# Chunks four to seven solved as two pairs on POOL, and their preparation and solving put above the weight conversions

## The chip, the cores and the metric

The kernel runs on one core of a Trainium2 chip. The core has five engines with a queue of their own each, and each takes its instructions strictly in the order in which they stand in that queue: TensorE (PE in the profile; its weight loads are PEld), VectorE (DVE), ScalarE (ACT), GpSimd (POOL) and SyncE (SP, which here only starts transfers). The metric is the device time of one execution in microseconds (us).

## The reference

Three layers follow each other. The first is a linear recurrence over 768 steps, for 4 x 8 = 32 heads with a 40 x 40 state each; the other two are feed-forward layers over the 3072 tokens that come out of it.

```python
for t in range(S):                                   # S = 768
    y[:, :, t] = einsum('bhd,bhde->bhe', r_t, state)
    Sa = einsum('bhde,bhe->bhd', state, a_t)
    state = state * w_t[:, :, None, :] - einsum('bhd,bhe->bhde', Sa, b_t) + einsum('bhd,bhe->bhde', v_t, k_t)
x = y as 3072 tokens x 320
h = x @ w_in                                         # 320 -> 2048
g = where(h >= 1, h, where(h <= -1, 0, (h + 1)**2 / 4))
x = g @ w_out                                        # 2048 -> 320
out = ((x @ w_a) * (x @ w_b)) @ w_out2               # 320 -> 1536 -> 320
```

Weights arrive as 64-bit floats and are taken apart on the chip into two 32-bit parts each, since a product is made of a high and a low part.

## The kernel before

**The recurrence** is cut into 24 chunks of 32 steps (C = 32). A chunk g passes through three routines:

- `prepare(g)` (line 113) needs no state, so it may run ahead. It loads `ein` (`load_e`), scans the decays on DVE (L127, L130), multiplies on POOL (L136, out `ein`), and multiplies on PE (L146, out `pab`) what DVE then masks into `lab` (L154); one part of it goes to DRAM as `amd` (L156). From chunk 4 on there is one buffer for `ein`, and the load of chunk g+1 is issued after the products of chunk g.
- A **solve** turns the 32 x 32 triangular matrix of each head of a chunk (`amd`) into its inverse (`xtd`). `solve(sb)` (line 203) does it for the four chunks of a block sb at once: 128 partitions are 4 chunks x 32 heads, and 30 rounds of two operations (L212 and L214, tiles `tm` and `apm`) run over all rows of the matrix. `solve_pair(i, eng)` (line 221) does it for two chunks, with the upper and the lower partitions each taking every second row: 31 rounds (L239, L241) over half as many rows. Before, chunks 0 and 1 are solved as a pair on DVE, chunks 2 and 3 as a pair on POOL, and all later ones in fours by `solve` on POOL.
- `core(g)` (line 285) carries the state on: products `pw` (L295), an ACT copy (`ws`, L298), products `pu` (L303) with the inverse `xtl` read back from `xtd` (`load_xt`), products `pss` (L314), whose result DVE scales into the next state (L317), and transposes `put` and `pst`. `outp(g)` and `x_out(g)` make the chunk's output and lay it into `xa`, the input of the first feed-forward layer, for two chunks at a time.

**The first feed-forward layer** (`ffn_block`, 12 blocks of two chunks) takes 16 pieces f a block: products `pha` (L588, L596), four operations on DVE, ACT and POOL, and products `ya`. It needs the converted weights. A **conversion** (`from_f64`, line 500) loads `raw`, and passes through DVE (L506, L507, L510, L511), ACT (L508, L509) and POOL (L512), then an ACT cast and a subtraction on POOL or DVE (L536, L546, L561). There are 36 of them for this layer. `p1_stage` (line 160) makes further tables for the chunks of a block, with two long scans on DVE (L178, L183) and two multiplications on POOL (L188, out `pkb`).

**The second feed-forward layer** (`pa`, `pb`, `po`) follows when the first is done.

**What sets the order:** the program is written as generators that a loop over chunks advances; a scheduler then puts every engine's instructions in order by a model of their times and by a priority, which is the place in the program moved by `tc.high_priority(offset=...)`. The conversions have an offset of -900 (line 447), the pieces of the first feed-forward layer -8000 (line 486); prepare, solve and core have none. The table `side` says beside which chunk a generator is advanced. The order is fixed when the program is built: on the chip an engine that waits for its next instruction does nothing else.

Of the kernel before, what the change touches and what calls it, by code (L numbers as in the profile page):

```python
# [16 lines left out]
C = 32  # L17
# [7 lines left out]
def rwkv_moe_kernel(ctx: ExitStack, tc: tile.TileContext, r, k, v, w, a, b, w_in, w_out, w2a, w2b, w2o, ein, pin, vin, rin, vtin, out):  # L25
# [44 lines left out]
    def recurrence(ffn_block, xap, spare, conv, more_units, early):  # L70
# [7 lines left out]
        with ExitStack() as es:  # L78
# [142 lines left out]
            def solve_pair(i, eng):  # L221
# [3 lines left out]
                t = pre.tile([128, CW], F32, name="apm") if i == 0 else spare("wi1", F32)[:, 0:CW]  # L225
                N = t[:, 0:C * C].rearrange("p (j i) -> p j i", i=C)
                X = t[:, 2:CW].rearrange("p (q i) -> p q i", i=2 * C + 2)[:, :, 0:C]
                nc.sync.dma_start(out=t[:, 0:C * C], in_=amd[0][2 * i:2 * i + 2].rearrange("c k q s t -> (c k q) (s t)").unsqueeze(0)
# [5 lines left out]
                tm = None if i == 0 else spare("wo1", F32)  # L234
                for m in range(C - 1):
                    n, k = C - 1 - m, m // 2 + 1
                    tv = (pre.tile([128, 240], F32, name="tm") if i == 0 else tm)[:, 0:k * n].rearrange("p (j i) -> p j i", i=n)
                    rows = X[:, n2 - k:n2]
                    eng.tensor_tensor(out=tv, in0=rows[:, :, m:m + 1].to_broadcast([128, k, n]),  # L239
                                            in1=N[:, m, m + 1:].unsqueeze(1).to_broadcast([128, k, n]), op=ALU.mult)  # L240
                    eng.tensor_tensor(out=rows[:, :, m + 1:], in0=rows[:, :, m + 1:], in1=tv, op=ALU.add)  # L241
                    if m % 2:
                        yield
                nc.gpsimd.affine_select(out=X, in_=X, pattern=[[2, n2], [1, C]], base=2 - C, channel_multiplier=0,
                                        compare_op=ALU.is_ge, fill=0.0)
                for h in range(2):
                    nc.sync.dma_start(out=xtd[0][2 * i:2 * i + 2].rearrange("c k q (j h) t -> h (c k q) j t", h=2)[h, :, ::-1],
                                      in_=X[64 * h:64 * h + 64])
# [36 lines left out]
            def core(g):  # L285

                ru, nxt, lab, wc = RU[g % 2], RU[(g + 1) % 2], LAB[g % PL], WC[g % (PL + 1)]
                if g % 4 == 0 or g == 2:
                    load_xt(g)
# [18 lines left out]
                if (g + 1) % 4 and g + 1 != 2:  # L308
                    load_xt(g + 1)
# [71 lines left out]


# [5 lines left out]
            for sb in range(1, NSB):  # L388
                gen = p1_stage(sb)
                slots = [4 * sb - 4 + j for j in range(4)]  # L390
                for j in slots:
                    put(j, 1, (gen, 3 if j < slots[-1] else 99))
                gen = solve(sb)
                for j in range(2):
                    put(4 * sb - 2 + j, 1, (gen, 9 if j < 1 else 99))
            for g in range(NCH):
                put(g + 2, 0, (x_out(g), 99))
                if g >= 4:
                    put(max(g - PL, (g - 4) // 2), 0, (prepare(g), 99))
# [631 lines left out]
```

## Time and profile before

| | us |
|---|---|
| median of 3 runs | 1519.99 (1517.62 to 1527.1) |
| profiled execution | 1516.01 |
| its span, from the first to the last instruction | 1514.0 |
| PE, DVE, ACT, POOL busy | 1124.2, 712.3, 522.0, 667.4 |
| granted clock of TensorE, mean over the span | 0.926 |

The span is the stretch that the trace covers; the profiled execution's own time is 2.0 us longer. A share of busy time is an average over stages that have different limits, so the stages have to be looked at one by one.

### The profile page before, as it was taken

What the parts mean: (1) busy time and instruction counts of PE and PEld (TensorE: products, weight loads), DVE (VectorE), ACT (ScalarE), POOL (GpSimd) and SP (SyncE); (2) the same over time, 40 slices, a digit from 0 to 9 for tenths busy, and PEclk for the clock granted to TensorE, in tenths of its full rate; (3) what the DMA queues carried; (4) which work ended last, traced back from release to release, by engine and by line L of the source; (5) the groups of instructions that cost most, each with busy time, mean ns of one, the idle gap of its engine ahead of it and who ended that gap; (6) DMA issues with size and microseconds to landing.
All of it is one profiled execution on the core that took longest, in us unless ns stands there. A gap on an engine that the chain in (4) does not pass through costs nothing.

```text
span 1514.0 us, 42965 instructions
## 1 busy us (share of the span) xinstructions
PE 1124.2 (74%) x18674; PEld 1005.5 (66%) x18674; DVE 712.3 (47%) x1345; ACT 522.0 (34%) x1171; POOL 667.4 (44%) x866
## 2 busy tenths in 40 slices
PE   0102234457676888887889978879999999999996
PEld 0102123356565778776778867779988888888885
DVE  5975677873444555546554366784411111111110
ACT  1212424244222333333444456565422222222221
POOL 4647455785082583285248235465422222222221
PEclk9999999988657998898889988989999999999998
DMA  8746778665645334534443243441110010000000
GB/s 232 136 129 124 156 155 188 157 141 107 152 123 139 91 106 114 138 97 102 106 130 107 80 137 113 133 129 44 52 30 21 19 37 23 18 1 18 1 18 20
DMA packets 193626, 144.72 MB, mean 96 GB/s; under 512 B 138644, under 2 KB 168340, under 8 KB 190932
## 3 DMA queue, kind: packets, MB, share of 16 engines
q1 hardware_dynamic: 160276, 128.25, 33.6%
q10 hardware_dynamic: 33152, 13.64, 4.0%
q8 instruction: 148, 2.42, 0.7%
q14 instruction: 50, 0.41, 0.1%
HBM read 111.97 MB, written 29.88 MB: 94 GB/s over the span
## 4 chain that ended last, share of the span: by engine, by line
PE 49%; DMA 16%; DVE 16%; POOL 8%; issue 6%; ACT 3%; SPq 1%; ACTq 0%; POOLq 0%; DVEq 0%
PE pb L596 9%; PE pa L596 8%; PE po L596 8%; DMA ein<-in_ein_dram 6%; PE pha L596 6%; PE ya L596 6%; POOL apm L214 2%; POOL tm L212 2%; DMA raw<-in_moe_w_in_dram 2%; DVE cve L506 1%; PE ya L588 1%; DVE cvf L511 1%; PE pss L314 1%; DVE ewx L127 1%; PE pha L588 1%
## 5 line engine op out<-in xcount | busy, mean ns | idle before, releaser
L650 POOL TENSOR_TENSOR gl<-cl,gh 128x256 fp32r<-128x256 f32 x192 | 144.5, 764 | 194.7 <-ACT gh L648 162.3
L701 POOL TENSOR_TENSOR gl<-gf,gh 128x512 fp32r<-128x512 f32 x72 | 92.8, 1289 | 308.4 <-ACT gh L699 308.4
L596 PE MATMUL pha<-xa,wi 128*128 128x256 f32 x1239 | 194.8, 302 | 0.8 <-issue 0.8
L697 DVE TENSOR_TENSOR gf<-pb,asb 128x512 f32<-128x512 f32 x72 | 49.7, 691 | 305.6 <-PE pb L596 297.2
L596 PEld LDWEIGHTS pha<-xa,wi 128*128 128x128 f32 x1239 | 179.8, 211 | 1.0 <-issue 1.0
L596 PE MATMUL ya<-wo,gh 128*128 128x320 f32 x576 | 138.2, 325 | 2.2 <-ACT yo L913 2.2
L644 ACT ACTIVATE cl<-cl 128x256 f32<-128x256 f32 x192 | 75.5, 416 | 168.7 <-DVE cl L643 166.6
L303 PE MATMUL pu<-ws,xtl 32*32 32x40 f32 x1536 | 28.1, 239 | 132.3 <-DMA xtl<-xtd 88.5
L512 POOL TENSOR_TENSOR cvf<-cvf,cve 128x256 f32<-128x256 f32 (+2 forms) x84 | 75.8, 902 | 114.6 <-DVE cve L510 66.9
L643 DVE TENSOR_SCALAR cl<-pha 128x256 f32<-128x256 f32 x177 | 69.2, 417 | 115.8 <-PE pha L596 106.6
L596 PE MATMUL ya<-wo,gl 128*128 128x320 f32 x384 | 111.3, 331 | 6.4 <-POOL gl L650 5.7
L303 PEld LDWEIGHTS pu<-ws,xtl 32*32 32x32 f32 x1536 | 23.8, 141 | 135.5 <-issue 97.0
L596 PE MATMUL po<-wo,gh 128*128 128x320 f32 x504 | 108.9, 308 | 0.0
L596 PEld LDWEIGHTS ya<-wo,gh 128*128 128x128 f32 x576 | 104.5, 204 | 3.8 <-ACT yo L913 2.5
L648 ACT CAST gh<-cl 128x256 fp32r<-128x256 f32 x192 | 74.5, 404 | 51.6 <-DVE cl L646 36.5
L699 ACT CAST gh<-gf 128x512 fp32r<-128x512 f32 x72 | 44.7, 621 | 133.9 <-DVE gf L697 131.8
L214 POOL TENSOR_TENSOR apm<-apm,tm 128x30 f32<-128x30 f32 (+9 forms) x150 | 86.9, 579 | 8.9
L596 PE MATMUL pb<-wi,w 128*128 128x512 f32 x288 | 90.8, 396 | 0.0
L596 PE MATMUL pb<-wo,w 128*128 128x512 f32 x288 | 90.7, 396 | 0.0
L695 ACT COPY asb<-pa 128x512 f32<-128x512 f32 x72 | 42.2, 587 | 133.7 <-PE pa L596 133.7
L212 POOL TENSOR_TENSOR tm<-apm 128x30 f32<-128x30 f32 (+9 forms) x150 | 82.0, 547 | 8.9
L646 DVE TENSOR_TENSOR cl<-pha,cl 128x256 f32<-128x256 f32 x177 | 70.1, 418 | 31.3 <-ACT cl L644 30.8
(167 smaller groups left out, 2598.8 us busy)
## 6 DMA issues: line engine op xcount, KB each, us to landing
ein<-in_ein_dram SPq DMA_DIRECT2D x21, 838.9 KB
vut<-in_vtin_dram SPq DMA_DIRECT2D x24, 416.0 KB
ru<-in_vin_dram SPq DMA_DIRECT2D x48, 160.0 KB
kbi<-pwd SPq DMA_DIRECT2D x48, 160.0 KB
lg<-pwd SPq DMA_DIRECT2D x48, 160.0 KB
pkb<-in_pin_dram SPq DMA_DIRECT2D x11, 640.0 KB
pwd<-pkb SPq DMA_DIRECT2D x11, 640.0 KB
ptw<-in_pin_dram SPq DMA_DIRECT2D x6, 660.5 KB
```

The source lines that it names most:

```text
L212: nc.gpsimd.tensor_tensor(out=tv, in0=X[:, 0:m, m:m + 1].to_broadcast([128, m, n]), in1=X[:, m, m + 1:].unsqueeze(1).to_broadcast([128, m, ...
L214: nc.gpsimd.tensor_tensor(out=X[:, 0:m, m + 1:], in0=X[:, 0:m, m + 1:], in1=tv, op=ALU.add)
L303: nc.tensor.matmul(pu[q:q + C, j, :], lhsT=xt[q:q + C, j, :], rhs=ws[q:q + C, j, :], start=True, stop=True)
L512: nc.gpsimd.tensor_tensor(out=f, in0=f, in1=e.bitcast(F32), op=ALU.mult)
L596: nc.tensor.matmul(**p)
L643: nc.vector.tensor_scalar(out=cl, in0=ph, scalar1=-1.0, scalar2=1.0, op0=ALU.max, op1=ALU.min)
L644: nc.scalar.activation(out=cl, in_=cl, func=AF.Square, scale=0.5, bias=0.5)
L646: nc.vector.tensor_tensor(out=gf, in0=ph, in1=cl, op=ALU.max)
L648: nc.scalar.copy(out=gh, in_=gf)
L650: nc.gpsimd.tensor_tensor(out=gl, in0=gf, in1=gh.bitcast(F32), op=ALU.subtract)
L697: nc.vector.tensor_tensor(out=gf, in0=pb, in1=asb, op=ALU.mult)
L701: nc.gpsimd.tensor_tensor(out=gl, in0=gf, in1=gh.bitcast(F32), op=ALU.subtract)
```

## The change

Chunks 4 to 7 are no longer solved by one `solve(1)`, but by two calls of `solve_pair` on POOL, the first for chunks 4 and 5, the second for 6 and 7; they use the tiles `apm` and `tm` of `solve`. The pair reads `amd` and writes `xtd` of its own block, so the first can start when two chunks are prepared, not four. `load_xt(6)` moves to the start of core(6). A new wrapper `ahead(gen, n)` advances a generator with a raised priority: 3000 for the two pairs, 1500 for the preparation of chunks 4 to 7.

```diff
--- before.py
+++ after.py
@@ -222,19 +222,20 @@
 
 
                 n2 = C // 2
-                t = pre.tile([128, CW], F32, name="apm") if i == 0 else spare("wi1", F32)[:, 0:CW]
+                sb, c = divmod(2 * i, 4)
+                t = pre.tile([128, CW], F32, name="apm") if i != 1 else spare("wi1", F32)[:, 0:CW]
                 N = t[:, 0:C * C].rearrange("p (j i) -> p j i", i=C)
                 X = t[:, 2:CW].rearrange("p (q i) -> p q i", i=2 * C + 2)[:, :, 0:C]
-                nc.sync.dma_start(out=t[:, 0:C * C], in_=amd[0][2 * i:2 * i + 2].rearrange("c k q s t -> (c k q) (s t)").unsqueeze(0)
+                nc.sync.dma_start(out=t[:, 0:C * C], in_=amd[sb][c:c + 2].rearrange("c k q s t -> (c k q) (s t)").unsqueeze(0)
                                   .to_broadcast([2, 64, C * C]))
                 yield
                 for h in range(2):
                     nc.gpsimd.memset(t[64 * h:64 * h + 64, C + h:C * (C - 1) + h + 1:2 * C], 1.0)
                 yield
-                tm = None if i == 0 else spare("wo1", F32)
+                tm = None if i != 1 else spare("wo1", F32)
                 for m in range(C - 1):
                     n, k = C - 1 - m, m // 2 + 1
-                    tv = (pre.tile([128, 240], F32, name="tm") if i == 0 else tm)[:, 0:k * n].rearrange("p (j i) -> p j i", i=n)
+                    tv = (pre.tile([128, 240], F32, name="tm") if i != 1 else tm)[:, 0:k * n].rearrange("p (j i) -> p j i", i=n)
                     rows = X[:, n2 - k:n2]
                     eng.tensor_tensor(out=tv, in0=rows[:, :, m:m + 1].to_broadcast([128, k, n]),
                                             in1=N[:, m, m + 1:].unsqueeze(1).to_broadcast([128, k, n]), op=ALU.mult)
@@ -244,7 +245,7 @@
                 nc.gpsimd.affine_select(out=X, in_=X, pattern=[[2, n2], [1, C]], base=2 - C, channel_multiplier=0,
                                         compare_op=ALU.is_ge, fill=0.0)
                 for h in range(2):
-                    nc.sync.dma_start(out=xtd[0][2 * i:2 * i + 2].rearrange("c k q (j h) t -> h (c k q) j t", h=2)[h, :, ::-1],
+                    nc.sync.dma_start(out=xtd[sb][c:c + 2].rearrange("c k q (j h) t -> h (c k q) j t", h=2)[h, :, ::-1],
                                       in_=X[64 * h:64 * h + 64])
                 yield
 
@@ -285,7 +286,7 @@
             def core(g):
 
                 ru, nxt, lab, wc = RU[g % 2], RU[(g + 1) % 2], LAB[g % PL], WC[g % (PL + 1)]
-                if g % 4 == 0 or g == 2:
+                if g % 4 == 0 or g in (2, 6):
                     load_xt(g)
                 xt = XT.pop(g)
                 quads = [(C * (2 * h + p), p, h) for h in range(2) for p in range(2)]
@@ -305,7 +306,7 @@
                 for q, p, h in quads:
                     nc.scalar.copy(out=ru[UR[p]:UR[p] + C, p, h::2], in_=pu[q:q + C])
                 yield
-                if (g + 1) % 4 and g + 1 != 2:
+                if (g + 1) % 4 and g + 1 not in (2, 6):
                     load_xt(g + 1)
                 for hs in halves:
                     ps = bank("pss", [128, HC, D])
@@ -379,6 +380,13 @@
                 nc.vector.tensor_tensor(out=xs[:, 3:6, :], in0=px, in1=xs[:, 0:3, :].bitcast(F32), op=ALU.subtract)
                 yield
 
+            def ahead(gen, n):
+                while True:
+                    with tc.high_priority(offset=n):
+                        if next(gen, NONE) is NONE:
+                            return
+                    yield
+
 
             side = {}
 
@@ -390,13 +398,17 @@
                 slots = [4 * sb - 4 + j for j in range(4)]
                 for j in slots:
                     put(j, 1, (gen, 3 if j < slots[-1] else 99))
+                if sb == 1:
+                    for i in range(2):
+                        put(i + 1, 1, (ahead(solve_pair(2 + i, nc.gpsimd), 3000), 99))
+                    continue
                 gen = solve(sb)
                 for j in range(2):
                     put(4 * sb - 2 + j, 1, (gen, 9 if j < 1 else 99))
             for g in range(NCH):
                 put(g + 2, 0, (x_out(g), 99))
                 if g >= 4:
-                    put(max(g - PL, (g - 4) // 2), 0, (prepare(g), 99))
+                    put(max(g - PL, (g - 4) // 2), 0, (ahead(prepare(g), 1500) if g < 8 else prepare(g), 99))
 
             def run(items):
                 for gen, n in items:
```

Three places show how the built order moves. Line numbers of the changed program are higher by 1 from the solve pair on and by 12 from the conversions on (L512 is L524, L561 is L573, L588 is L600).

**POOL, where the solve of chunk 4 begins.** `cvf<-cvf,cve` is a conversion, `ein<-ein` a preparation, `tm` and `apm` the solve. Before:

```order
L512 TENSOR_TENSOR cvf<-cvf,cve 128x256
L136 TENSOR_TENSOR ein<-ein 104x1024
L512 TENSOR_TENSOR cvf<-cvf,cve 128x320
L561 TENSOR_TENSOR wo_722<-cvf,wo_722 128x320
L512 TENSOR_TENSOR cvf<-cvf,cve 128x256
L536 TENSOR_TENSOR wi_723<-cvf,wi_723 128x2x128
L212 TENSOR_TENSOR tm<-apm 128x30
L214 TENSOR_TENSOR apm<-apm,tm 128x30
L212 TENSOR_TENSOR tm<-apm 128x58
```

Of the change:

```order
L548 TENSOR_TENSOR wi_719<-cvf,wi_719 128x2x128
L136 TENSOR_TENSOR ein<-ein 104x1024
L524 TENSOR_TENSOR cvf<-cvf,cve 128x320
L233 MEMSET apm 64x16 x2
L240 TENSOR_TENSOR tm<-apm 128x31
L573 TENSOR_TENSOR wo_720<-cvf,wo_720 128x320
L242 TENSOR_TENSOR apm<-apm,tm 128x31
L240 TENSOR_TENSOR tm<-apm 128x30
L242 TENSOR_TENSOR apm<-apm,tm 128x30
L524 TENSOR_TENSOR cvf<-cvf,cve 128x256
L240 TENSOR_TENSOR tm<-apm 128x58
L242 TENSOR_TENSOR apm<-apm,tm 128x2x29
```

Before, all of the solve stood behind 28 of the 36 conversions on POOL. Now the first pair begins behind 16 and ends behind 29, with 13 conversions and the preparations of chunks 7 and 8 between its rounds; the second begins behind 32 and ends after all 36. The preparations of chunks 5, 6, 7, 8 and 9 stand behind 12, 15, 21, 24 and 29 conversions, where they stood behind 15, 20, 23, 26 and 31.

**POOL, the end of the solve of chunks 8 to 11** (`L217` sets its diagonal, `gl` belongs to the first feed-forward layer). Before:

```order
L217 MEMSET apm 128x32
L214 TENSOR_TENSOR apm<-apm,tm 128x28x3
L212 TENSOR_TENSOR tm<-apm 128x58
L214 TENSOR_TENSOR apm<-apm,tm 128x29x2
L212 TENSOR_TENSOR tm<-apm 128x30
L214 TENSOR_TENSOR apm<-apm,tm 128x30
L136 TENSOR_TENSOR ein<-ein 104x1024
L650 TENSOR_TENSOR gl<-cl,gh 128x256
```

Of the change:

```order
L212 TENSOR_TENSOR tm<-apm 128x84
L217 MEMSET apm 128x32
L214 TENSOR_TENSOR apm<-apm,tm 128x28x3
L136 TENSOR_TENSOR ein<-ein 104x1024
L212 TENSOR_TENSOR tm<-apm 128x58
L662 TENSOR_TENSOR gl<-cl,gh 128x256 x2
L214 TENSOR_TENSOR apm<-apm,tm 128x29x2
L212 TENSOR_TENSOR tm<-apm 128x30
L214 TENSOR_TENSOR apm<-apm,tm 128x30
```

The `ein` in both pieces is the preparation of chunk 14: before it stood behind the whole solve, now it stands ahead of the solve's last five operations.

**PE, around the start of chunk 4** (`pw<-ru_176,lab_164`). Before:

```order
L332 MATMUL pst<-ident,ru_177 40x40 x16
L295 MATMUL pw<-ru_176,lab_164 32x40 x32
L346 MATMUL pg<-rg,vut 32x32 x64
L588 MATMUL pha<-xa,wi_717 128x256
L596 MATMUL pha<-xa,wi_717 128x256 x7
```

Of the change:

```order
L600 MATMUL pha<-xa,wi_717 128x256
L608 MATMUL pha<-xa,wi_717 128x256 x7
L296 MATMUL pw<-ru_176,lab_164 32x40 x32
L347 MATMUL pg<-rg,vut 32x32 x37
L304 MATMUL pu<-ws,xtl 32x40 x32
L347 MATMUL pg<-rg,vut 32x32 x27
L373 MATMUL px<-ident,ys 128x128 x3
```

Before, the 16 pieces of the first feed-forward block all stood between `pw` and `pu` of chunk 4. Now two of them stand ahead of `pw`, and `pu` follows `pw` with only `pg` between; counted at the `pu` of chunks 5, 6, 7 and 8, 3, 5, 9 and 19 pieces have had their `pha`. From the `pu` of chunk 10 on the count is within three pieces of the one before at every chunk (30 and 28 at chunk 10, 60 and 60 at chunk 14, 107 and 107 at chunk 20). On ACT, the `ws` of chunks 1, 2, 3 and 4 stands behind 15, 24, 29 and 35 conversions, where it stood behind 18, 26, 31 and 36.

## Rows read from the trace of the kernel before

**Rows 1.** The page, part 2: busy tenths in 40 slices of 37.8 us, and granted clock.
```profile
PE   0102234457676888887889978879999999999996
...
PEclk9999999988657998898889988989999999999998
```

**Rows 2.** Windows; columns: stretch, length, busy PE, PEld, DVE, ACT, POOL, clock, DMA.
```profile
182.00:260.00 78.00, 28.90 (x1046) 24.92 (x1050) 61.30 (x97) 28.62 (x60) 38.70 (x28) 1.00 0.77 170
312.00:372.00 60.00, 40.93 (x416) 37.67 (x416) 30.11 (x54) 25.60 (x51) 47.90 (x56) 0.86 0.62 116
372.00:466.00 94.00, 58.40 (x2295) 51.19 (x2299) 35.52 (x60) 22.05 (x49) 39.80 (x68) 0.57 0.55 135
466.00:939.00 473.00, 406.85 (x9627) 370.14 (x9621) 259.99 (x559) 194.99 (x492) 227.08 (x358) 0.89 0.42 111
```

**Rows 3.** Chain that ended last, 355 to 470 us; columns: start, us, what.
```profile
362.74 4.97 DMA xtd<-apm
...
367.74 4.87 DMA xtl<-xtd
...
372.65 1.29 PE pu L303 x64
...
404.30 6.60 DMA ein<-in_ein_dram
...
465.74 1.29 PE pu L303 x64
```

**Rows 4.** Timeline of PE; columns: start, us, instruction, count, idle time before and its end.
```profile
176.23 1.94 PE L146 MATMUL pab<-lab,ein 40*32 40x32 f32 x128 [20.48 <-POOL ein L136]
...
233.19 1.93 PE L146 MATMUL pab<-lab,ein 40*32 40x32 f32 x128 [11.23 <-POOL ein L136]
...
312.19 1.30 PE L295 MATMUL pw<-ru,lab 128*32 128x40 f32 x64 [3.08 <-ACT lg L333]
...
430.20 1.29 PE L303 MATMUL pu<-ws,xtl 32*32 32x40 f32 x64
...
446.30 1.08 PE L146 MATMUL pab<-lab,ein 40*32 40x32 f32 x64
```

**Rows 5.** Timeline of POOL, 178 to 457 us.
```profile
178.64 0.87 POOL L512 TENSOR_TENSOR cvf<-cvf,cve 128x320 f32<-128x320 f32 x1 [1.78 <-DVE cve L510]
...
259.99 0.24 POOL L212 TENSOR_TENSOR tm<-apm 128x30 f32<-128x30 f32 x1
...
269.49 3.33 POOL L512 TENSOR_TENSOR cvf<-cvf,cve 128x256 f32<-128x256 f32 x1
...
279.86 3.07 POOL L214 TENSOR_TENSOR apm<-apm,tm 128x210 f32<-128x210 f32 x1
...
326.58 0.86 POOL L561 TENSOR_TENSOR wo<-cvf,wo 128x320 fp32r<-128x320 f32 x1
...
415.31 2.18 POOL L136 TENSOR_TENSOR ein<-ein 104x1024 f32<-104x1024 f32 x1 [13.53 <-DVE ein L130]
417.45 0.23 POOL L212 TENSOR_TENSOR tm<-apm 128x30 f32<-128x30 f32 x1
...
456.49 0.26 POOL L214 TENSOR_TENSOR apm<-apm,tm 128x30 f32<-128x30 f32 x1
```

**Rows 6.** The pair on POOL by its tile `wi`; columns: duration ns min/median/max, first, last start.
```profile
L239 POOL TENSOR_TENSOR wo<-wi x31: 236/377/2745, 104.9 to 141.3; 128x126 f32<-128x126 f32 x3, 128x30 f32<-128x30 f32 x2, 128x56 f32<-128x56 f32 x2, 128x78 f32<-128x78 f32 x2
L241 POOL TENSOR_TENSOR wi<-wi,wo x31: 232/377/452, 105.2 to 144.2; 128x126 f32<-128x126 f32 x3, 128x30 f32<-128x30 f32 x2, 128x56 f32<-128x56 f32 x2, 128x78 f32<-128x78 f32 x2
```

**Rows 7.** Timeline of DVE, 278.5 to 283 us.
```profile
279.29 3.26 DVE L183 TENSOR_TENSOR_SCAN ptw<-ptw,crp 128x1321 f32<-128x1321 f32 x1
```

**Rows 8.** Waits, 150 to 480 us; columns: waiting <- awaited, us in total, times, longest.
```profile
DVE ewx L127 <- DMA ein<-in_ein_dram: 43.0, 6, 16.1
POOL ein L136 <- DVE ein L130: 41.2, 3, 15.1
```

## Prediction

> **What bounds the kernel now.** I read the page first. The slices show PE nearly idle at the start, half busy in the slices from about 300 to 490 us, and at 8 or 9 tenths from there on; the granted clock dips to 5 tenths in the same stretch [rows 1]. The windows give sizes: PE is busy 406.85 of 473 us between 466 and 939, which leaves little to win there, but only 58.40 of 94 between 372 and 466, at a granted clock of 0.57, that is mostly at the lower of its two levels [rows 2]. So what is lost on PE is lost before 466 us, and the question is what holds the chunks up until then.
>
> The chain of waits names it. It passes through the rounds of a solve on POOL to `xtd<-apm`, 4.97 us, `xtl<-xtd`, 4.87 us, and only then the `pu` of chunk 4 at 372.65 [rows 3]. The `pw` of the same chunk had been ready at 312.19 [rows 4]: chunk 4 stood for 60.5 us and waited for its solve. In that time PE did the whole first feed-forward block, so the 60 us are not simply lost: 40.93 of 60 were busy [rows 2]. But after it the chunks ran alone at 19.2 us each ((430.20 - 372.65) / 3) [rows 3, 4] and there was no feed-forward work to fill them with.
>
> Why the solve is late is seen on POOL. Its first round starts at 259.99 [rows 5], because it needs four prepared chunks and stands behind 28 conversions, and its rounds then share POOL with the last conversions, the last of which ends at 326.58 + 0.86 [rows 5]. Between 182 and 260 us POOL is busy for 38.70 of 78 us: there is room [rows 2].
>
> **The pairs on POOL.** The solve of chunks 8 to 11, which shares POOL with little else, takes 417.45 to 456.49 + 0.26, or 39.3 us [rows 5]. A pair is 31 + 31 operations at a median of 377 ns, 23.4 us; this removes one solve and adds two pairs, 46.7 us, so POOL gets about 8 us more in all [rows 5, 6]. By its order the first pair begins after the 16th conversion, which POOL ran at 178.64, and ends after the 29th, at 269.49 [rows 5]. It needs 23.4 us of room, of which the window up to 260 us has 39. I take its end as 272, when that conversion ended with its 3.33 us, provided the conversions keep their pace. Adding 4.97 and 4.87 for the two transfers, `xtl` is there at 282, well before chunk 4 wants it. Everything of the added load of `amd` and of `xtd` stays off the path as long as that margin of about 20 us stands; SP's queue has the load of `xtl` behind the first pair's `xtd` and the second pair's load, and I put that inside the margin.
>
> **The preparations.** PE stood idle for 20.48 us before the `pab` of chunk 5 and 11.23 us before that of chunk 7, each time with a `pw` queued behind it and POOL's `ein` as the releaser [rows 4]. Raising the preparations can take between nothing and 31.7 us off the way to chunk 4. In the built order the `ws` of chunk 4 is one conversion further ahead than before and that of chunk 1 three; conversions 16 to 36 took 148 us, 7.4 us each [rows 5], so 7 to 22 us. I take 10, near the lower end, since the wait for the load of `ein` itself, 43.0 us over six times, stays [rows 8]. Chunk 4's `pw` comes at 302.
>
> **Chunk 4 to chunk 8.** Two feed-forward pieces now stand ahead of that `pw`. A piece costs at most 40.93 / 16 = 2.6 us of PE with what stood beside it, about 2.3 without [rows 2]; two are 4.6, and the `pw` itself is 1.30 [rows 4]. ACT's copy between `pw` and `pu` I leave to the bounds. So `pu` of chunk 4 is at 308 instead of 372.65: 64 us earlier. The 16 pieces that covered this wait must now run among chunks 4 to 7. If none is hidden, chunk 8's `pu` is at 308 + 4 x 19.2 + 16.5 x 2.3 = 423.
>
> The solve of chunks 8 to 11 becomes the next wait. In the new order its last five operations stand on POOL behind the `ein` of chunk 14, whose load is issued after the `pab` of chunk 13, in chunk 7. With `pu` of chunk 7 at 375 (half of 8 pieces hidden) to 384 (none), that `pab` ends 17.2 us later (446.30 + 1.08 - 430.20 [rows 4]) plus 6 to 11 for five pieces between; from the issue of the load to the end of POOL's `ein` it is 13.2 us (404.30 to 415.31 + 2.18 [rows 3, 5]); the five operations take 1 us and the transfers 9.8 [rows 3]. That gives 422 to 436, and I take 429 where it was 465.74 [rows 3]: 37 us earlier. From chunk 10 on the order holds the same pieces per chunk, and PE is busy for 86% of that stretch [rows 2], so what is gained at chunk 8 is carried to the end.
>
> **The sum.** Span 1514.0 - 37 = 1477; the profiled execution is 2 us above its span, so 1479. The median of the runs shown is 4 us above the profiled execution, so 1483.
>
> A rule speaks against putting these rounds on POOL. A POOL round operation took 3.07 us at 279.86 where its neighbours take about 0.6, and a DVE scan of two inputs ran from 279.29 for 3.26 us; both ended together, at 282.93 and 282.55 [rows 5, 7]. The Trainium skill, SBUF — State Buffer, section "Who interferes with whom", says why: a DVE instruction with two SBUF inputs and a GpSimd instruction that reads SBUF exclude each other, and the second to issue waits for all of the first. On that rule the trace agrees. If it decided, the sum would be the 1506 of the second rival; where the room on POOL takes it up, it is 1483.
>
> **Rivals.** *More.* If the preparations give their 22 us and the last solve isn't held by chunk 14, chunk 8 comes at 423 - 12 = 411, 55 us earlier: 1465. For it: the 20.48 us wait. Against it: the order on POOL.
>
> *POOL and DVE hold each other.* In 182 to 330 us DVE is the busier engine, 61.30 of 78 [rows 2]. Each preparation brings two scans and each table stage two; a held operation loses up to 2.5 us (3.07 less 0.6) [rows 5]. Nine such holds more than before, one for each of five preparations and four scans, cost 23 us on both queues, conversions slip by as much, and chunk 4 with them: a gain of 14, 1506. Against it: the removed solve met such holds too.
>
> *Slower: the conversions wait in POOL's queue.* POOL's order is fixed. A raised preparation that reaches the queue's head before its `ein` is loaded and scanned stops the conversions behind it, then DVE and ACT, whose queues hold the state's copies behind conversions 15 to 35. POOL waited for such a scan three times for 41.2 us, at worst 15.1, and DVE for the load six times [rows 8]. Five preparations at 15.1 us are 75; the gain of 37 is gone from 7.4 us each on, and at the worst the time is 1520 + 38 = 1558. Against it: the order of transfers has these loads early too, and a short wait takes the room that POOL has anyway.
>
> That the change doesn't do what it says is in part so: 13 conversions still stand inside the first pair. If it ended 20 us later than I take it, chunk 4 would still not wait.
>
> **Chances and range.** The forecast has 0.53, and holds 1460 to 1500 with its bounds (chunk 4 between 290 and 312, and 422 to 436 at chunk 8). More has 0.18, the holds 0.18, slower 0.11. A measurement of this kernel tells about 1% from no change, here 15 us. Faster by over 1%, below 1505: the forecast, more, and a little of the holds, 0.72. Within 1%: 0.17. Slower: 0.11. The range from 1455 to 1514 leaves out the slower case and the ends of the others.
>
> **What would show it.** Right: `pu` of chunk 4 within 10 us of its `pw`, near 308, and of chunk 8 near 429; the first pair's last round near 272; PE busier between 300 and 430 and a higher granted clock there. The step on the pace is wrong if POOL's last conversion ends after 345; the one on chunk 8 if its `pu` waits for `xtl` past 440; and the carrying to the end if chunk 8 comes early but chunk 20 doesn't.

## The result and the profile after

The changed kernel takes 1502.26 us (median of 3 runs, 1502.19 to 1504.69) where the kernel before took 1519.99: a ratio of 0.9886, 95% interval 0.9857 to 0.9915, 17.7 us faster. The forecast was 1483, 37 us faster. The direction was right and less than half of the size came. By the spans of the profiled executions it is 13.5 us of the 37; the 4 us that the forecast added for the median over the profiled execution did not appear (1502.26 against 1502.19).

The page of the changed kernel, part 2, answers to [rows 1]; its span is 1500.5 us, the mean granted clock 0.896:

```profile
PE   0102314455688888788789978889999999999996
...
PEclk9999955555888999988899988899999999999998
```

PE's row is hardly changed. The clock is at 5 tenths from 188 to 375 us, behind a stretch in which PE was busy for 3 tenths or less; before, it fell to 6 and 5 only between 378 and 454, though PE had been as idle at the start [rows 1]. The forecast's sign of being right, a busier PE at a higher clock from 300 to 430, did not come: PE was busy for 84 us instead of 88, at 0.67 instead of 0.75. Windows of the changed kernel, columns as in [rows 2]:

```profile
182.00:260.00 78.00, 24.62 (x931) 21.13 (x931) 57.66 (x88) 26.92 (x55) 53.62 (x74) 0.58 0.72 165
312.00:372.00 60.00, 30.98 (x1092) 27.11 (x1092) 34.01 (x55) 21.58 (x45) 42.94 (x66) 0.57 0.87 175
372.00:466.00 94.00, 71.70 (x1731) 65.51 (x1721) 40.80 (x81) 27.27 (x68) 51.83 (x84) 0.82 0.48 109
466.00:939.00 473.00, 399.21 (x9576) 361.34 (x9563) 260.51 (x556) 195.87 (x493) 226.78 (x358) 0.91 0.42 113
```

Between 312 and 372 PE is busy for 31 us instead of 41, between 372 and 466 for 72 instead of 58: the feed-forward work left the first stretch and came back in the second. The timeline of PE, as in [rows 4]:

```profile
228.47 1.93 PE L146 MATMUL pab<-lab,ein 40*32 40x32 f32 x128 [21.85 <-POOL ein L136]
...
305.92 0.58 PE L600 MATMUL pha<-xa,wi 128*128 128x256 f32 x1
...
309.63 1.04 PE L296 MATMUL pw<-ru,lab 128*32 128x40 f32 x64
...
315.96 1.29 PE L304 MATMUL pu<-ws,xtl 32*32 32x40 f32 x64 [4.51 <-ACT ws L299]
...
348.25 1.29 PE L304 MATMUL pu<-ws,xtl 32*32 32x40 f32 x64 [5.09 <-ACT ws L299]
...
365.49 0.98 PE L333 MATMUL pst<-ident,ru 40*40 40x40 f32 x16 [7.93 <-ACT vut L327]
...
387.49 1.54 PE L304 MATMUL pu<-ws,xtl 32*32 32x40 f32 x64 [8.48 <-DMA xtl<-xtd]
...
409.92 0.77 PE L304 MATMUL pu<-ws,xtl 32*32 32x40 f32 x62
...
457.04 1.29 PE L304 MATMUL pu<-ws,xtl 32*32 32x40 f32 x64 [2.42 <-DMA xtl<-xtd]
...
478.26 0.79 PE L304 MATMUL pu<-ws,xtl 32*32 32x40 f32 x64
```

These are `pab` of chunk 7, the first of two feed-forward pieces, `pw` and `pu` of chunk 4, `pu` of chunk 5, `pst` of chunk 5, and `pu` of chunks 6, 7, 8 and 9. Chunk 4's `pu` comes 56.7 us earlier than before [rows 3], chunk 7's 20.3, chunk 8's 8.7. From `pu` of chunk 4 to that of chunk 8 it was 93 us before and is 141 now. The last `ya` of the first layer comes 13.8 us earlier (1102.6 to 1088.8), the end 13.5 by the spans.

POOL, as in [rows 5]: first and last operation of the first pair, last conversion, last of the second pair, and the solve of chunks 8 to 11 with the `ein` of chunk 14 ahead of its last five operations:

```profile
192.06 0.29 POOL L233 MEMSET apm<- 64x16 f32 x2 [7.79 <-DMA apm<-amd]
...
281.13 1.09 POOL L245 TENSOR_SCALAR_AFFINE_SELECT apm<-apm 128x512 f32<-128x512 f32 x1
...
334.25 0.87 POOL L573 TENSOR_TENSOR wo<-cvf,wo 128x320 fp32r<-128x320 f32 x1
...
367.89 0.72 POOL L245 TENSOR_SCALAR_AFFINE_SELECT apm<-apm 128x512 f32<-128x512 f32 x1
...
389.30 0.59 POOL L212 TENSOR_TENSOR tm<-apm 128x30 f32<-128x30 f32 x1 [20.70 <-DMA apm<-amd]
...
442.44 2.20 POOL L136 TENSOR_TENSOR ein<-ein 104x1024 f32<-104x1024 f32 x1 [3.74 <-DVE ein L130]
...
447.82 0.26 POOL L214 TENSOR_TENSOR apm<-apm,tm 128x30 f32<-128x30 f32 x1
```

### The profile page after: what moved, and what is told of

It reads as the page before. It is cut to its first block, busy times and chain, and to the rows that moved or that the text cites. A ratio compares the mean times of both kernels' runs of the same rounds, so it can differ in the third digit from the quotient of the medians.

```text
span 1500.5 us, 43009 instructions
## 1 busy us (share of the span) xinstructions
PE 1113.6 (74%) x18674; PEld 995.2 (66%) x18674; DVE 714.0 (48%) x1345; ACT 521.8 (35%) x1171; POOL 677.8 (45%) x935
## 5 line engine op out<-in xcount | busy, mean ns | idle before, releaser
L524 POOL TENSOR_TENSOR cvf<-cvf,cve 128x256 f32<-128x256 f32 (+2 forms) x84 | 68.4, 814 | 105.8 <-DVE cve L522 49.8
L608 PEld LDWEIGHTS po<-wo,gh 128*128 128x128 f32 x504 | 83.3, 188 | 2.0
L608 PE MATMUL pa<-wi,w 128*128 128x512 f32 x252 | 82.3, 396 | 0.0
```

The lines of the kernel that those rows point to most:

```text
L524: nc.gpsimd.tensor_tensor(out=f, in0=f, in1=e.bitcast(F32), op=ALU.mult)
L608: nc.tensor.matmul(**p)
```

## The experiments

Every ratio is against the kernel before, run on the same chip in the same session. The times of chunks come from the one profiled execution of each kernel, which lies up to 8 us from its median (p5out_before and h3 above it, h5 below).

**Each half alone.** The pairs without the raised preparations, and the raised preparations with the solve of four:

```diff
 # e1: the pairs stay
-                    put(..., (ahead(prepare(g), 1500) if g < 8 else prepare(g), 99))
+                    put(..., (prepare(g), 99))
 # e2: the solve of four is back, and load_xt(6) where it was
-                if sb == 1:
-                    for i in range(2):
-                        put(i + 1, 1, (ahead(solve_pair(2 + i, nc.gpsimd), 3000), 99))
-                    continue
```

> Only the two pairs, and the preparations of chunks 4 to 7 back at their old priority. Theory (the pairs remove the 60 us wait of chunk 4 for the solve of four; what the preparations' priority gains at chunk 1 is lost again at chunk 7's preparation): pu of chunk 4 between 314 and 324, time 1498 to 1512, most of the gain is here. Rival (the preparations' priority is what costs: the POOL queue held by an unready preparation, 21.85 us of idle PE ahead of chunk 7's pab): faster than the whole change, 1485 to 1495. Second rival (the priority brings the gain by itself): 1512 to 1520.

> Only the priority of the preparations of chunks 4 to 7; the solve of four for chunks 4 to 7 as before. Theory: pw of chunk 4 comes 0 to 5 us earlier than 312, its pu still waits for the whole solve and comes at 360 to 373: 1508 to 1520. Rival (the preparations' priority costs by itself): above 1522. Rival (it brings most of the 17 us): 1500 to 1507.

The pairs alone: 1.0037 (1.0012 to 1.0062), a little slower than before. The preparations alone: 0.9929 (0.9902 to 0.9955), 11 us faster, inside the range expected but with chunk 4's `pw` 15 us earlier instead of 0 to 5 and its `pu` at 353 instead of 360 to 373. Both theories fell: most of the gain is in the preparations, as the second rival of e1 had it (which expected 1512 to 1520 of the pairs; they took 1525). `pw` and `pu` of chunk 4 in the two kernels, pairs alone first:

```profile
326.06 1.29 PE L296 MATMUL pw<-ru,lab 128*32 128x40 f32 x64
332.52 1.29 PE L304 MATMUL pu<-ws,xtl 32*32 32x40 f32 x64 [4.07 <-ACT ws L299]
```

```profile
297.31 1.29 PE L296 MATMUL pw<-ru,lab 128*32 128x40 f32 x64
...
352.90 0.79 PE L304 MATMUL pu<-ws,xtl 32*32 32x40 f32 x64 [1.56 <-DMA xtl<-xtd]
...
451.95 1.29 PE L304 MATMUL pu<-ws,xtl 32*32 32x40 f32 x64 [12.81 <-DMA xtl<-xtd]
```

`pw` was at 312.19 [rows 4]. The preparations bring 15 us, and with the pairs `pw` is 12 to 14 us later (312 to 326, 297 to 309.6). Of the 12, 3.7 are the two feed-forward pieces that PE takes ahead of it in the changed kernel, from 305.92 on. With the preparations alone chunk 4 still waits to 353, 37 us longer than in the changed kernel, and yet chunk 8 comes at 452, 5 us earlier than there. So an early chunk 4 is worth little.

**Less and more of the pairs on POOL.** The second pair cut to four of its 31 rounds (the rest of the solve of chunks 6 and 7 is left out); the rounds of both pairs on DVE; chunks 8 to 11 as pairs too.

```diff
 # p2cut
-                for m in range(C - 1):
+                for m in range(4 if i == 3 else C - 1):
 # bdve
-                        put(i + 1, 1, (ahead(solve_pair(2 + i, nc.gpsimd), 3000), 99))
+                        put(i + 1, 1, (ahead(solve_pair(2 + i, nc.vector), 3000), 99))
 # x1_pairs811 (load_xt also at the start of core(10))
-                if sb == 1:
+                if sb <= 2:
-                        put(i + 1, 1, (ahead(solve_pair(2 + i, nc.gpsimd), 3000), 99))
+                        put(4 * sb - 3 + i, 1, (ahead(solve_pair(2 * sb + i, nc.gpsimd), 3000), 99))
```

> The changed kernel, with the second pair's solve cut to its first four rounds (the other 28 rounds of chunks 6 and 7 are left out), so that POOL is free of some 60 operations between 310 and 368. Theory (chunk 6 waits 8.5 us for the second pair; chunks 4 and 5 are slow for their own reasons): pu of chunk 6 from 387 to 376 to 380, chunks 4 and 5 as they are (pu 316 and 348, within 3 us), pu of chunk 8 from 457 to 444 to 450, time 1490 to 1496. Rival (POOL's rounds hold DVE and the chain, which makes chunks 4 and 5 slow): pu of chunk 5 at 340 or earlier, pu of chunk 8 below 440, time 1475 to 1488. Rival (the wait is hidden by what follows): 1500 to 1505.

> The changed kernel with the rounds of both pairs on DVE in place of POOL. Theory (the pairs' 124 rounds on POOL hold the preparation of chunk 7, the conversions and the preparations of the next chunks, which takes back most of what the pairs bring): pab of chunk 7 at 218 to 224 (228 to 231 now), pw of chunk 4 at 296 to 303 (309.6 now), time 1480 to 1497. Rival (DVE, the engine busiest until 312, becomes the bound; 62 rounds at 0.42 us a pair are 26 us each): pw of chunk 4 after 315, time above 1510.

> The changed kernel, with chunks 8 to 11 solved as two pairs as well. Theory (the step from chunk 7 to chunk 8, 47 us, is the wait for the solve of four that stands behind chunk 11's and 13's preparations; what chunk 8 gains stays to the end): pu of chunk 8 from 457 to 428 to 440, time 1474 to 1488. Rival (PE, filled with feed-forward pieces or at the lower clock, sets the pace from chunk 7 on): pu of chunk 8 earlier, but the time 1497 to 1505. Rival (POOL has no room for a pair's 66 operations beside the preparations and becomes the bound): 1505 to 1525.

The cut pair: 0.9919 (0.9887 to 0.9951). 27 rounds are left out, not 28. Chunk 6 came at 376 and chunk 8 at 443, close to the theory, and the time is no better than with the whole pair, as the last rival had it. On DVE: 0.9883 (0.9848 to 0.9919), the same as the change; `pw` of chunk 4 at 313 and `pab` of chunk 7 at 227.8 are hardly earlier or later than with the rounds on POOL (309.6 and 228.5), and not at 296 to 303 and 218 to 224 as the theory said. Pairs for 8 to 11: 1.0184 (1.0125 to 1.0242), the third theory refuted: chunk 8 came at 468.5. PE and POOL of that kernel show why:

```profile
459.07 0.64 PE L608 MATMUL ya<-wo,gl 128*128 128x320 f32 x1 [13.47 <-POOL gl L662]
```

```profile
457.84 0.29 POOL L233 MEMSET apm<- 64x16 f32 x2 [15.14 <-DMA apm<-amd]
458.29 0.72 POOL L662 TENSOR_TENSOR gl<-cl,gh 128x256 fp32r<-128x256 f32 x1 [0.17 <-POOL apm L233]
```

The second of those pairs reached the head of POOL's queue 15 us before its matrix was there. Behind it stood the `gl` of a feed-forward piece, PE waited for that, and behind PE's piece stood `pw` of chunk 8.

**What the old wait covered.** Three pairs of kernels, each the kernel before and the changed one: with 11 of the 14 matmuls left out in every piece of the first feed-forward block (n; the expectations say 17 of 20, which counts a piece too large); without the arithmetic of the last table stage, `p1_stage(5)` (p5out); without both (np). A fourth, y2, has no pairs and raises the preparations of chunks 4 to 11.

```diff
 # n: in_proj and out_proj of block 0
+            seq = seq[0:1]         # and in out_proj only gh times the high part
 # p5out: p1_stage
+                if sb == NSB - 1:      # loads, pwd and wtd as they are; no scans, no L188, no L194 to L200
 # y2
-                    ... (ahead(prepare(g), 1500) if g < 8 else prepare(g), 99))
+                    ... (ahead(prepare(g), 1500) if g < 12 else prepare(g), 99))
```

> The kernel before, with the first of the twelve feed-forward blocks cut to 3 of its 20 matmuls a piece (17 of 20 left out in those 16 pieces). By the trace some eleven pieces run while chunk 4 waits for the solve of four. Theory (the wait was not idle: feed-forward pieces filled two thirds of it): that filling goes and chunk 4 waits as long as before, pu of chunk 4 at 368 to 375 and of chunk 8 at 455 to 467. Alone it tells nothing; with the next run it gives what the change is worth when the wait cannot be filled.

> The changed kernel with the same cut of the first feed-forward block. Theory (what the wait used to hold has to run between chunks 4 and 8 now, so the gain is only the idle part of the wait): without these matmuls pu of chunk 8 comes 25 to 40 us earlier than in the kernel before with the same cut (uncut: 9 us), and the end 22 to 38 us earlier (uncut: 13.5). Rival (chunks 4 to 7 are slow by themselves, held by conversions, by POOL's rounds and by their own chain of copies): the two differ at chunk 8 and at the end by no more than 17 us.

> No pairs; preparations of chunks 4 to 11 (not only 4 to 7) with the priority above the conversions. Theory (the gain of the preparations is that the solve of four starts earlier, and chunks 8 to 11 already have room): within 5 us of the run with chunks 4 to 7 alone, 1503 to 1516. Rival (the solve for chunks 8 to 11 is what holds chunk 8, and earlier preparations lift it): pu of chunk 8 from 452 to below 443, time 1493 to 1502.

> The kernel before without the arithmetic of the last table stage (chunks 20 to 23): its scans, its two products on POOL, its copies and sums on ACT are left out, its transfers stay. Theory (the stage ran under chunk 4's wait): chunk 4's pu still waits for the solve of four, 360 to 372 (372.7 with the stage), pu of chunk 8 455 to 465 and the time 1505 to 1520, the little that there is coming from 7 us of POOL inside the solve.

> The changed kernel without the arithmetic of the last table stage, as in the run before this one. Theory (that stage, no longer covered by the wait, is what holds chunks 5 and 6 by 11.67 us on ACT and about 11 us on POOL): pu of chunk 8 from 457 to 425 to 437, the two kernels without the stage differ by 22 to 40 us at chunk 8 (9 with it) and by 25 to 40 at the end. Rival (what chunk 8 gains is not kept, because feed-forward pieces that did not run by then have to run later): chunk 8 as the theory says, but the end differs by 8 to 20. Rival (the stage is not the cause): chunk 8 at 450 or later.

> The kernel before with both kinds of work left out that ran under chunk 4's wait: 17 of 20 matmuls of the first feed-forward block's pieces, and the arithmetic of the last table stage. Theory: the wait stays, now empty: pu of chunk 4 at 355 to 368, of chunk 8 at 450 to 462, time 1510 to 1525.

> The changed kernel with the same two left out. Theory (what the wait covered is all that took the gain): chunk 8's pu at 405 to 428, 30 to 45 us before that of the kernel before with the same cuts, and the end 27 to 45 us earlier. Rival (chunks 4 to 8 are held by their own preparations and by the solve of chunks 8 to 11 on POOL, whatever PE has to do): chunk 8 at 432 to 445, the two differ by 10 to 22 us at chunk 8 and at the end. Rival (what chunk 8 gains is lost again behind it in any case): 30 us or more at chunk 8, under 22 at the end.

| left out | before | changed | difference | `pu` of chunk 8, before and changed |
|---|---|---|---|---|
| nothing | 1519.99 | 1502.26 | 17.7 | 465.7, 457.0 |
| first block's matmuls (n) | 1530.63 | 1507.31 | 23.3 | 471.8, 455.5 |
| last table stage (p5out) | 1506.48 | 1503.76 | 2.7 | 457.0, 441.2 |
| both (np) | 1515.00 | 1510.03 | 5.0 | 451.2, 442.3 |

Ratios to before: n 1.0042 (1.0021 to 1.0062) and 0.9898 (0.9868 to 0.9928), p5out 0.9896 (0.9864 to 0.9928) and 0.9881 (0.9843 to 0.9919), np 0.9970 (0.9946 to 0.9993) and 0.9936 (0.9911 to 0.9961), y2 0.9942 (0.9910 to 0.9974). The cover is not what took the gain. Without the feed-forward matmuls the steps of the changed kernel are the same within 4 us (chunks 4 to 8 at 313, 348, 384, 407, 455); the two kernels differ by 16 us at chunk 8, as the rival of n has it, and by 23 at the end, at the foot of the theory's 22 to 38. Without both, 9 us at chunk 8 and 5 at the end are left, which none of the three had. y2 is near e2, as its theory had it (chunk 8 at 457). The table stage does hold chunks 6 to 8, as the next runs show too, but without it the end stays. And leaving it out of the kernel before brings 14 us, near the best that was expected (1505 to 1520); the profiled execution of that kernel took 1514.68, so its 457.0 belongs to an execution 8 us longer than the median. POOL of the kernel before, in the solve of chunks 4 to 7:

```profile
342.70 3.60 POOL L188 TENSOR_TENSOR pkb<-pkb,ptw 128x1280 f32<-128x1280 f32 x1
...
355.99 3.59 POOL L188 TENSOR_TENSOR pkb<-pkb,ptw 128x1280 f32<-128x1280 f32 x1 [0.96 <-DMA pkb<-in_pin_dram]
...
362.45 0.27 POOL L214 TENSOR_TENSOR apm<-apm,tm 128x30 f32<-128x30 f32 x1
```

The stage's two products, for chunks that run 450 us later, stood inside the solve that chunk 4 waited for. In the changed kernel they run behind the `pu` of chunk 4. Leaving the whole stage out brings nearly as much time, and the two gains do not add.

**The table stages moved.** Held behind what SP has to issue ahead of their own place in the program: the last stage (h5), the last three (h3), the same three without the change (h3_before) and with the pairs on DVE (h3d); then only ACT's part of the last stage, with the pairs on POOL (h5a) and on DVE (h5ad).

```diff
+            def held(gen):
+                while True:
+                    with tc.issue_after(last(SP)):
+                        if next(gen, NONE) is NONE:
+                            return
+                    yield
-                gen = p1_stage(sb)
+                gen = held(p1_stage(sb)) if sb >= 5 else p1_stage(sb)    # h5; >= 3 in h3, h3_before, h3d
 # h5a, h5ad: L194 alone, in p1_stage(5), and so what follows it
+                with tc.issue_after(last(ACT)):
                     nc.scalar.activation(out=tw, in_=tw, func=AF.Abs, accum_out=...)
```

> The changed kernel with the last table stage (for chunks 20 to 23) issued behind chunk 15 in place of beside chunks 4 and 5. Theory (chunks 4 to 7 are slow since work for later chunks, which used to run under chunk 4's wait, now stands ahead of theirs in the in-order queues; here ACT's 11.67 us wait for this stage's product ahead of chunk 5's copy, and 11 us of POOL inside the second pair): pst of chunk 5 from 365.5 to 354 to 359, pu of chunk 6 from 387.5 to 370 to 380, pu of chunk 8 from 457 to 444 to 452, time 1488 to 1498. Rival (PE with its feed-forward pieces and its low clock sets the pace): no step moves by more than 3 us, 1500 to 1505. Rival (the stage costs as much where it now stands): chunk 8 earlier, the end not.

> The changed kernel with the last three table stages (chunks 12 to 23) each held until four chunks before its use. Theory: each stage takes about 7 us of DVE, 7 of POOL and 5 of ACT out of the crowded stretch from 200 to 370; pw of chunk 4 from 309.6 to 295 to 304, pu of chunk 8 to 436 to 447, time 1475 to 1492. Rival (conversions alone fill that stretch, the stages are cover): pw of chunk 4 within 4 us, time 1497 to 1505. Rival (held stages meet the feed-forward at chunks 8 to 20): above 1505.

> The kernel before, with the same three table stages held. Theory (before, the stages ran under chunk 4's wait and beside the conversions, so that taking them out only lets the solve of four start some microseconds earlier): pu of chunk 4 from 372.7 to 358 to 370, time 1505 to 1519; the whole change is then worth 20 to 40 us against this kernel, more than the 17.7 without the hold. Rival (the stages cost the same in both): the difference between the two held kernels is 17 us or less.

> The changed kernel with the last three table stages held and the rounds of both pairs on DVE. Theory (both take work out of the queues in which chunks 3 to 7 wait): pu of chunk 4 at 300 to 313, of chunk 8 at 425 to 440, time 1465 to 1485. Rival (DVE becomes the bound beside the conversions): pu of chunk 4 above 316, time as h3 or slower. Rival (the solve of four for chunks 8 to 11 is the floor): pu of chunk 8 at 440 to 450 whatever chunk 7 does.

> The changed kernel with only ACT's part of the last table stage (two sums, one copy and the transfers behind it) issued behind chunk 19; its scans and its two products on POOL stay where they are. Theory (ACT's 11.67 us wait holds chunk 5, POOL's share holds the second pair and so chunk 6): pst of chunk 5 from 365.5 to 354 to 360, pu of chunk 6 from 387.5 to 377 to 386, pu of chunk 8 to 444 to 453, time 1490 to 1500. Rival (only the stage as a whole matters, or only POOL's part): chunk 6 at 386 or later, 1499 to 1506.

> The changed kernel with the rounds of both pairs on DVE and ACT's part of the last table stage behind chunk 19. Theory: POOL's share of the stage no longer meets the second pair; pu of chunk 8 from 448.6 (pairs on DVE alone) to 436 to 446, time 1480 to 1496. Rival (chunk 8 is held by its own solve of four): pu of chunk 8 within 4 us of 448.6, time 1494 to 1505.

| | ratio, interval | `pu` of chunks 8, 9 | last `ya` |
|---|---|---|---|
| h5 | 0.9964 (0.9939 to 0.9990) | 430.5, 460.3 | 1095.3 |
| h3 | 0.9964 (0.9945 to 0.9982) | 415.3, 451.4 | 1109.5 |
| h3_before | 0.9867 (0.9810 to 0.9924) | 419.7, 448.0 | 1087.7 |
| h3d | 1.0103 (1.0066 to 1.0141) | 423.1, 462.0 | 1117.0 |
| h5a | 0.9912 (0.9879 to 0.9946) | 436.5, 465.7 | 1089.8 |
| h5ad | 1.0002 (0.9980 to 1.0023) | 443.8, 479.0 | 1110.4 |

In h5 chunk 8 comes where the forecast had it, and the end does not follow. `pu` of chunks 6 and 8 in h5:

```profile
369.92 1.29 PE L304 MATMUL pu<-ws,xtl 32*32 32x40 f32 x64 [3.48 <-ACT ws L299]
...
430.54 1.29 PE L304 MATMUL pu<-ws,xtl 32*32 32x40 f32 x64
```

All six times lie outside what their theories gave. The stages seem to cost their time again where they then stand (the third rival of h5): from chunk 9 to the last `ya` it is 635 to 658 us with held stages and 610 to 631 in all other kernels but x1 (638). The kernel before with three stages held is as fast as the change, though its chunks 4 to 7 are solved in one and no priority is raised. With the three stages held the change is a loss, 1515.3 (h3) against 1501.9 (h3_before), where it was expected to be worth 20 to 40 us. No version is clearly faster than the change: h3_before, bdve and the change lie inside each other's intervals.

## Why the prediction was wrong

**The pairs: mis-sized, and their loads put at nothing.** The first pair ended at 282.2 where 272 was forecast, and its `xtl` was there in time; the last conversion slipped by 7.7 us. But the sum put the added load of `amd` off the path, and it stood ahead of chunk 7's preparation in the queue of SP. The changed kernel, then e2, which has no pairs; columns: start, us, what SP issues:

```profile
179.13 0.56 SPq L229 DMA_DIRECT2D apm<-amd  x1
...
181.05 10.69 SPq L267 DMA_DIRECT2D xtl<-xtd  x1
...
197.80 0.75 SPq L115 DMA_DIRECT2D ein<-in_ein_dram  x1
```

```profile
181.79 1.55 SPq L267 DMA_DIRECT2D xtl<-xtd  x1
...
190.18 0.34 SPq L115 DMA_DIRECT2D ein<-in_ein_dram  x1
```

Behind the first pair's load the issue of `xtl` took 10.69 us instead of 1.55, so `ein` of chunk 7 was asked for 7.6 us later than in e2, and its `pab` came 8.0 us later (228.47 against 220.44). With the rounds on DVE it was the same (10.39 us, `pab` at 227.8). From the issue of that `ein` to the `pab` it was 30 us in e2 (30.3), the change (30.7) and bdve (29.2), so there the pairs cost what their load costs, and not their rounds. In all twelve kernels with the pairs and the raised preparations an issue of SP behind that load took 9.3 to 10.8 us (in e1 one behind the second pair's load, 9.3); in the seven that solve chunks 4 to 7 in one, no issue of SP took more than 6. No run moves this load alone, so what it costs at the end stays open.

The rounds also took more than 46.7 us. By the tile `apm`, columns as in [rows 6]:

```profile
L240 POOL TENSOR_TENSOR tm<-apm x62: 220/388/2880, 192.4 to 367.3; 128x126 f32<-128x126 f32 x6, 128x30 f32<-128x30 f32 x4, 128x56 f32<-128x56 f32 x4, 128x78 f32<-128x78 f32 x4
L242 POOL TENSOR_TENSOR apm<-apm,tm x62: 228/407/2923, 193.4 to 367.6; 128x126 f32<-128x126 f32 x6, 128x30 f32<-128x30 f32 x4, 128x56 f32<-128x56 f32 x4, 128x78 f32<-128x78 f32 x4
```

Grouped by line the two are busy for 30.1 and 31.3 us together, 61.4. The longest answers to [rows 5, 7]; POOL, then DVE:

```profile
338.34 2.92 POOL L242 TENSOR_TENSOR apm<-apm,tm 128x126 f32<-128x126 f32 x1
```

```profile
338.15 2.91 DVE L178 TENSOR_TENSOR_SCAN pwx<-ptw,crp 128x1321 f32<-128x1321 f32 x1 [2.74 <-DMA ptw<-in_pin_dram]
```

The round lasts as long as the scan and ends 0.2 us behind it. The Trainium skill, SBUF — State Buffer, section "Who interferes with whom", says that such a pair exclude each other; the trace agrees. The second rival was real, at most 15 us of POOL (61.4 less 46.7), but not what decided: on DVE the rounds gave the same time.

**The preparations: right alone, smaller with the pairs.** 10 us were forecast ahead of the two pieces; e2 shows 15, the changed kernel 6.3 (312.19 to 305.92). The 20.48 us ahead of `pab` of chunk 5 fell to 7.3, and the 11.23 ahead of chunk 7's grew to 21.85. In e2 they grew to 16.45; the rest is the late load of `ein`.

**Chunk 4 to chunk 8: the step that failed.** `pu` of chunk 4 was to come at 308 and came at 316. From there to `pu` of chunk 7 the forecast had 67 to 76 us (19.2 a chunk and some pieces) and it took 94. The pace was read from a stretch in which only chunks ran, and the forecast added nothing to it but the pieces. Moved 57 us forward, chunks 4 to 6 run beside the last conversions, the last table stage, the second pair and the preparations of chunks 10 and 11, and queues hold them in turn. DVE and ACT of the changed kernel:

```profile
322.59 1.26 DVE L127 TENSOR_TENSOR_SCAN ewx<-ein,cre 104x529 f32<-104x529 f32 x1 [5.99 <-DMA ein<-in_ein_dram]
...
332.12 0.98 DVE L318 TENSOR_TENSOR ru<-pss,wc 40x320 f32<-40x320 f32 x2
```

```profile
363.57 1.31 ACT L194 ACTIVATE ptw<-ptw 128x1321 f32<-128x1321 f32 x1 [11.67 <-POOL pkb L188]
364.78 0.19 ACT L194 ACTIVATION_READ_ACCUMULATOR ptw<-ptw 128x1 f32 x1
364.87 0.56 ACT L327 COPY vut<-put 40x512 f32<-40x512 f32 x1
```

DVE waits 6 us for the load of chunk 10's `ein` ahead of chunk 4's state; ACT waits 11.67 for a table of chunks 20 to 23 ahead of chunk 5's copy, and PE's `pst` with it; chunk 6 waits 8.48 for the second pair. Runs show the second and the third as far as chunk 6: with ACT's part moved it came at 380 (h5a), with the cut pair at 376, instead of 387.5. But chunk 7 came at 405 and 413, where the change has it at 410, so neither sets the pace. The first is read from the trace only.

What set the pace is seen by taking the way from `pu` of chunk 4 to that of chunk 7 in the other runs. It took 94 us as well without the first block's matmuls (n_after) and with the second pair cut (p2cut), so neither the matmuls of the pieces nor the rounds of that pair made it long; 89 and 81 with the last table stage left out or held (p5out_after, h5), and 74 with three stages held (h3), inside the forecast's range. In h3 POOL's last conversion also ends 33 us earlier than in the change. So the term left at nothing is, for the larger part, the table stages and the conversions that they delay; their shares were not separated.

**Chunk 7 to chunk 8: right.** From `pab` of chunk 13 (ending at 431.3) to `pu` of chunk 8 it was 25.7 us, forecast 24, with chunk 14's `ein` where it was named. The wait for `xtl` past 440, which the forecast named as a sign against this step, came because chunk 7 was late. The forecast did not look at another distance: in all 19 kernels that solve chunks 8 to 11 in one, `pu` of chunk 8 comes 61.5 us or more after chunk 11's `pab` (61.5 before, 89.6 in the change, 70 to 73 in h5, h5a, p2cut and np_after), whose result that solve needs. That `pab` ends at 367.5 in the changed kernel; by the smallest distance seen, chunk 8 would come there at 429 at the earliest, the forecast's own number.

**The carry to the end: right here, wrong as a rule.** In the changed kernel 8.7 us at chunk 8 became 13.8 at the last `ya`. But p5out_after has chunk 8 16 us earlier than the change and ends with it. The feed-forward matmuls suggest why: up to chunk 8 the trace has 224 before, 248 in the change, 150 in p5out_after. In the change, from chunk 4's `pw` to chunk 8's `pu` (columns as in [rows 2] without ACT and POOL, then without DVE and POOL; `pha`, then `ya`):

```profile
309.63:457.04 147.41, 23.53 (x137) 21.23 (x136) 14.92 (x38) 0.72 0.66 141
```

```profile
309.63:457.04 147.41, 20.76 (x96) 17.15 (x96) 0.41 (x1) 0.72 0.66 141
```

That is 44.3 us for 233, 0.19 each. At this price the change is 8.7 us and 24 matmuls ahead at chunk 8, 13.3 us together, near the 13.8 of the last `ya`; p5out_after is 16 us ahead of the change but owes 98 matmuls, 18.6 us. Counted so, the last `ya` comes out within 4 us of the trace in e1, e2, p2cut and h5a too, but up to 19 us too early in other kernels (y2, x1, h5ad), so this is an account read from the traces that no run tests. It also fits that leaving 176 matmuls out brought the changed kernel nothing: nearly all of them ran ahead of chunk 8, and behind it the trace has as many in both (2322 and 2319).

So the step that failed is the pace from chunk 4 to chunk 7, 94 us where 67 to 76 were forecast: chunk 4 was 8 us late, chunk 8 28 us (457 against 429). That an earlier chunk 8 is carried to the end held here, and fails as a rule.

**The rivals.** "More" and "slower" did not come. The time lies near the 1506 of the holds, and inside the forecast's wide range, for other reasons: that is luck.

**What stays open.** The versions that do all the work and beat the kernel before by 0.7% or more lie between 1501 and 1511 whichever wait they remove. That chunk 9, followed by 610 us or more, is the floor fits all of them; what would bring chunk 9 and its pieces forward together was not found, and the spread behind chunk 9 (610 to 631 us without held stages) is explained only as far as the owed matmuls go.

## What to carry to other kernels

Moving a chain forward puts it beside whatever ran ahead of it, so its pace must not be read from a stretch where it ran alone: here 58 us for three chunks became 94. With queues in a fixed order, look in the wait for work that is needed much later; here leaving out the stage whose two products stood inside the solve brought nearly as much as the pairs with the preparations. Look at the queue that issues loads as well: one load added there delayed another by 7.6 us. Measure an early milestone by time and by the work done up to it, and try each half of a change alone.

## What the runs showed of the hardware

In this stretch of small matmuls the granted clock made no difference. Up to chunk 5 x1 has the order of the changed kernel on PE, but its clock stayed at the level of 2.4 GHz to 312 us:

```profile
182.00:260.00 78.00, 27.18 (x931) 23.34 (x931) 59.71 (x89) 28.38 (x57) 54.55 (x74) 1.00 0.71 161
260.00:312.00 52.00, 25.50 (x731) 21.85 (x735) 38.81 (x54) 19.27 (x40) 30.44 (x44) 1.00 0.67 162
```

In the change it was mostly at that of 1.2 GHz (0.58 and 0.52 in the two windows). PE is busy for 52.7 us in x1 and 51.6 in the change, and `pu` of chunk 4 comes at 318.3 and 316.0. And leaving 176 matmuls out of the kernel before made it slower (1.0042), not faster: chunk 4 waited from 313.1 to 375.7, no shorter than before, and the order behind it was another.
